# Three fixed expert tiles instead of two, and small moves among the attention steps, in a fused attention and mixture-of-experts kernel

## The chip, the cores and the metric

The kernel runs on one core of a Trainium2 chip. The metric is the device time of one execution in microseconds. PE is the matrix engine (PEld its weight loads), DVE the vector engine, ACT the scalar engine, POOL GpSimd, and SP the engine that issues most transfers.

## The reference

Three stages follow one another. In the attention stage each head projects q and k by `w_phi`, subtracts the row maximum of the absolute value, takes exp of both signs, and forms the linear attention quotient. The output, 4608 tokens by 512, feeds a top-1 mixture of eight experts behind a skip score, and that feeds a feed-forward layer.

```python
kv = np.einsum('bhsf,bhsd->bhfd', k_p, v)
z = np.sum(k_p, axis=2)
num = np.einsum('bhsf,bhfd->bhsd', q_p, kv)
den = np.einsum('bhsf,bhf->bhs', q_p, z)[..., None] + 1e-06
...
do_compute = x @ w_skip > 0
e_idx = np.argmax(xc @ w_gate, axis=1)
h = np.maximum(xc[mask] @ w1[e], 0.0)
out = xc + gate_w * (h @ w2[e])
...
h = x @ w_in
return (h - np.tanh(h)) @ w_out
```

How many tokens an expert gets depends on the inputs, which are drawn from a fixed seed.

## The kernel before, in words

The instructions of each engine stand in the order in which the program is written; nothing reorders them.

**Attention** (L695 to L787) runs 32 steps, numbered 0 to 31: a step is half the tokens of a pair of batches for one pair of heads, and eight steps finish a pair of batches. In step i the next step's keys are projected (`project(n, "k")`, L699), then the maximum is subtracted on DVE (`shift`, L250), the queries are transposed, keys and values multiplied (L305), and the key sums turned into columns (`key_value_1`, L319). The key sums themselves are eight adds a step on POOL (`key_sum`, L277 to L280), made one step ahead. Then come the next queries' projection, `key_value_t` (L327, into the same PSUM tile `kvb`), and the numerators (L343); DVE divides a step later. Both projections write one PSUM tile, `proj`, from a pool with one buffer, so each waits for the shift before it. Every second step also turns a slice of 64-bit weights into 32-bit ones (`narrow`, on DVE, ACT and POOL).

**Routing** of a pair of batches is spread over the eight steps after it, called phases. Phase 1 picks the expert, phase 2 computes the gate and the rank (`route_gate`, `route_rank`, ending in a scan, `cum`, L420, and three small operations), phase 3 counts (`route_count`, two matmuls into `kvb` at L451 and L452, two adds on DVE) and computes slots. Phases 3, 4 and 5 store the token rows into per-expert segments, three indexed stores a phase (`scatter`, L473, on POOL's queue). The last pair's routing comes after attention.

**First expert.** In step 28 (`first_expert`, L499) the expert with most tokens so far is chosen, so that its first 256 rows can be run while the last pair is still being routed. Its weights, `raw`, are split into a high part (ACT, `wh`) and a remainder (`wl`), quarter by quarter (`wsplit`, L98); in steps 29 to 31 the remainders stand on POOL.

**Fixed stage** (L855 to L901). Two tiles of 128 rows run in straight code: `up` is 24 matmuls in two halves of 512 columns, `relu_t` transposes and splits, `down` is 24 matmuls. Among them stand the last pair's gate, rank, count, slots and nine indexed stores, a table of the tiles left (`block_table`, on DVE), and the load of the loop's first rows.

**Loop** (L899). Each remaining tile is one turn; the number of turns is read from the table. A turn multiplies a tile, transposes the next tile's rows (L106) and loads the one after it. At an expert's first tile its weights are split. Then the feed-forward layer follows (L1000, L1016).

## Time and profile before

| | |
|---|---|
| runs of the kernel before, median of 3 | 1479.0 us (1476.55 to 1480.41) |
| profiled execution | 1478.13 us |
| its span, first to last instruction | 1476.4 us |
| granted PE clock, mean over the span | 0.973 of full |
| busy: PE, DVE, ACT, POOL | 1402.8 us (95%), 699.8 us (47%), 556.1 us (38%), 394.8 us (27%) |

A row of a timeline is one run of like instructions: its start, its duration, the engine and line, what it writes and reads, and in brackets how long the engine had been idle and what released it. Busy time of PE is not time at full rate, so the granted clock has to be read beside it. PE can work at full clock (1.00) or at half.

### The profile page before, as it was taken

The numbers are of one execution on the slowest core, as the hardware profiler recorded it, in microseconds if no ns is written. First come the engines' busy times: TensorE is split into PE (matmuls) and PEld (weight loads), VectorE is DVE, ScalarE is ACT, GpSimd is POOL, SyncE is SP. The second block draws the span as 40 slices with busy tenths as digits, with TensorE's granted clock in tenths as the row PEclk, the third lists the DMA queues.
The fourth block names the chain that finished last, engine by engine and source line by source line (L and its number), as shares of the span: only waits on it lengthen the run. The fifth ranks groups of instructions, "written<-read, shape, count | busy, mean of one in ns | idle before, by whom it ended". The sixth has DMA issues, their size and how long they took to land.

```text
span 1476.4 us, 26209 instructions
## 1 busy us (share of the span) xinstructions
PE 1402.8 (95%) x9733; PEld 1157.2 (78%) x9733; DVE 699.8 (47%) x1081; ACT 556.1 (38%) x911; POOL 394.8 (27%) x417
## 2 busy tenths in 40 slices
PE   6999999998999999869999999999999999999998
PEld 5887787876778777748888888888888888888886
DVE  4788787786624453557852322323223232232322
ACT  4676565655313241436642222322223222222321
POOL 4776866868601120252330100101001010000000
PEclk9999999999899999978999999999999999999999
DMA  5753765846641422334330010101001010000000
GB/s 176 181 190 126 263 218 175 270 147 211 237 164 39 153 84 101 124 132 169 123 115 0 20 39 0 57 1 57 0 0 58 0 57 1 0 29 1 29 0 30
DMA packets 53875, 139.58 MB, mean 95 GB/s; under 512 B 5776, under 2 KB 5904, under 8 KB 50704
## 3 DMA queue, kind: packets, MB, share of 16 engines
q1 hardware_dynamic: 47440, 116.16, 23.9%
q0 software_dynamic: 5760, 18.90, 4.3%
q10 hardware_dynamic: 576, 3.15, 0.5%
q8 instruction: 69, 1.13, 0.3%
q14 instruction: 30, 0.25, 0.1%
HBM read 86.00 MB, written 52.19 MB: 94 GB/s over the span
## 4 chain that ended last, share of the span: by engine, by line
PE 49%; DVE 2%; POOL 2%; issue 1%; ACT 1%; DMA 0%; POOLq 0%
PE h L1000 24%; PE acc L1016 24%; POOL raw L216 1%; PE xtr L989 1%; DVE wol L96 1%; DVE raw L213 1%; ACT woh L95 1%; POOL raw L958 0%; DVE raw L209 0%; DMA raw<-x2s,gidx 0%; DVE raw L197 0%; DVE wl L96 0%; ACT raw L205 0%; DVE raw L200 0%; DVE g L1004 0%
## 5 line engine op out<-in xcount | busy, mean ns | idle before, releaser
L1004 DVE TENSOR_TENSOR g<-h,g 128x512 f32<-128x512 f32 x144 | 99.4, 690 | 389.8 <-ACT g L1003 389.8
L1003 ACT ACTIVATE g<-h 128x512 f32<-128x512 f32 x144 | 85.7, 595 | 391.5 <-PE h L1000 391.5
L1000 PE MATMUL h<-x2Th,wh 128*128 128x512 f32 (+1 forms) x580 | 226.0, 390 | 0.0
L1000 PE MATMUL h<-x2Tl,wh 128*128 128x512 f32 (+1 forms) x580 | 225.7, 389 | 0.0
L1000 PE MATMUL h<-x2Th,wl 128*128 128x512 f32 (+1 forms) x580 | 225.7, 389 | 0.0
L1016 PE MATMUL acc<-woh,gh 128*128 128x512 f32 x576 | 225.6, 392 | 0.0
L1016 PE MATMUL acc<-woh,gl 128*128 128x512 f32 x576 | 224.3, 389 | 0.0
L1016 PE MATMUL acc<-wol,gh 128*128 128x512 f32 x576 | 224.1, 389 | 0.0
L958 POOL DMA_INDIRECT raw<-x2s,gidx x36 | 35.4, 982 | 428.2 <-PE xtr L989 416.1
L96 DVE TENSOR_TENSOR gl<-g,gh 128x512 fp32r<-128x512 f32 x144 | 101.0, 702 | 98.9 <-ACT gh L95 98.9
L95 ACT CAST gh<-g 128x512 fp32r<-128x512 f32 x144 | 89.5, 622 | 110.8 <-DVE g L1004 110.8
L1000 PEld LDWEIGHTS h<-x2Th,wh 128*128 128x128 f32 x580 | 110.0, 190 | 22.3
L1000 PEld LDWEIGHTS h<-x2Th,wl 128*128 128x128 f32 x580 | 109.9, 189 | 22.4
L1000 PEld LDWEIGHTS h<-x2Tl,wh 128*128 128x128 f32 x580 | 110.0, 190 | 22.2
L1016 PEld LDWEIGHTS acc<-woh,gl 128*128 128x128 f32 x576 | 108.1, 188 | 22.6
L1016 PEld LDWEIGHTS acc<-wol,gh 128*128 128x128 f32 x576 | 108.2, 188 | 21.9
L1016 PEld LDWEIGHTS acc<-woh,gh 128*128 128x128 f32 x576 | 108.1, 188 | 21.9
L96 POOL TENSOR_TENSOR wl<-raw,wh 128x1024 fp32r<-128x1024 f32 x25 | 65.4, 2644 | 205.8 <-PE y L832 202.6
L292 ACT ACTIVATE qp<-tq 128x640 f32<-128x640 f32 (+1 forms) x128 | 76.3, 648 | 53.8 <-PE tq L286 52.6
L343 PEld LDWEIGHTS num<-kv,qp 128*64 128x64 f32 x2304 | 87.2, 139 | 8.2 <-ACT kv L332 7.4
L343 PE MATMUL num<-kv,qp 128*64 128x74 f32 x2304 | 92.4, 234 | 0.6
L277 POOL TENSOR_TENSOR ks<-ke 128x256 f32<-128x256 f32 x64 | 52.2, 816 | 69.3 <-ACT ke L265 69.1
(193 smaller groups left out, 2243.5 us busy)
## 6 DMA issues: line engine op xcount, KB each, us to landing
raw<-in_wall_dram SPq DMA_DIRECT2D x20, 1024.0 KB, 6.4
raw<-in_w_dram SPq DMA_DIRECT2D x30, 512.0 KB, 3.6
x2s<-raw SPq DMA_DIRECT2D x24, 512.0 KB, 6.9
out_dram<-raw SPq DMA_DIRECT2D x36, 256.0 KB, 4.1
x2s<-x SPq DMA_DIRECT2D x9, 768.0 KB
k<-in_kT_dram SPq DMA_DIRECT2D x16, 320.0 KB, 2.9
q<-in_qT_dram SPq DMA_DIRECT2D x16, 320.0 KB, 4.8
v<-in_vx_dram SPq DMA_DIRECT2D x16, 320.0 KB
```

What stands on the lines that cost most here:

```text
L95: nc.scalar.copy(hi, src)
L96: eng.tensor_tensor(out=lo, in0=src, in1=hi.bitcast(F32), op=ALU.subtract)
L213: nc.vector.tensor_tensor(out=x, in0=x, in1=m, op=ALU.add)
L216: nc.gpsimd.tensor_tensor(out=x, in0=x, in1=e.bitcast(F32), op=ALU.mult)
L277: g.tensor_tensor(out=t, in0=k[:, :, 0, s], in1=k[:, :, 1, s], op=ALU.add)
L292: nc.scalar.activation(qp[h][:, s, :n], t[:, :n], AF.Exp, scale=1.0 - 2.0 * s)
L343: nc.tensor.matmul(num[r : r + 64, h, c], qp[h][:, s, slot, r : r + 64], kv[:, s, h], start=s == 0, stop=s == 1,)
L958: nc.gpsimd.indirect_dma_start(out=xg[:, t, :], out_offset=None, in_=x2s[:, :], in_offset=bass.IndirectOffsetOnAxis(ap=gidx[:, b * TB + t ...
L1000: nc.tensor.matmul(p[:, s], a[:, o : o + P], b[:, k, s], start=n == 0, stop=n == 11)
L1003: nc.scalar.activation(g, p, AF.Tanh)
L1004: nc.vector.tensor_tensor(out=g, in0=p, in1=g, op=ALU.subtract)
L1016: nc.tensor.matmul(acc[t], a[:, s], b[:, m], start=m == 0 and n == 0, stop=m == NM - 1 and n == 2)
```

## The change

1. The fixed tiles of the first expert are three (`EARLY`, `NEARLY` = 384). The third tile's rows come into `xu`; two offsets are read in place of one; the PSUM tile of the row transposes and the tiles `r`, `hh`, `hl`, `xTh`, `xTl` grow by a tile.
2. In phase 3 the counts stand behind the next queries' projection instead of ahead of the shift of the keys.
3. For the first two routed pairs the nine indexed stores are spread over phases 3 to 7 as 2, 2, 2, 2 and 1; for the third they stay at three a phase.
4. The four remainders of the first expert's up weights in steps 29 to 31 stand on DVE.
5. The fixed stage is written in another order: both halves of the second tile's up product ahead of the counts, the third tile's behind them, and the last quarter's remainder of the down weights earlier.

```diff
 W = D + 1
-NEARLY = 256
+EARLY = 3
+NEARLY = EARLY * P
 MAXT = 48
...
     bx = rctx.enter_context(tc.tile_pool(name="rows", bufs=1, side="right"))
-    xTh = bx.tile([P, 2, 4, P], F32R, name="xTh")
-    xTl = bx.tile([P, 2, 4, P], F32R, name="xTl")
+    xTh = bx.tile([P, EARLY, 4, P], F32R, name="xTh")
+    xTl = bx.tile([P, EARLY, 4, P], F32R, name="xTl")
     xr = bx.tile([P, W], F32, name="xr")
...
     forced = rt.tile([P, E], F32, name="forced")
-    head = rt.tile([P, 4], F32, name="head")
-    headi = rt.tile([P, 4], I32, name="headi")
+    head = rt.tile([P, 5], F32, name="head")
+    headi = rt.tile([P, 5], I32, name="headi")
     tab = rt.tile([P, 7], F32, name="tab")
...
         src = st[i][w]
-        p = st[i]["p" + w] = pp.tile([P, NCH * 2, NF], F32, name="proj")
+        p = st[i]["p" + w] = pp.tile([P, 12, NF], F32, name="proj")
         for c in range(4):
...
         v.tensor_scalar(
-            out=head[:, 3:4], in0=head[:, 1:2], scalar1=-float(P), scalar2=0.0, op0=ALU.add, op1=ALU.max
+            out=head[:, 4:5], in0=head[:, 1:2], scalar1=-float(P), scalar2=0.0, op0=ALU.add, op1=ALU.max
+        )
+        v.tensor_scalar(
+            out=head[:, 3:4], in0=head[:, 4:5], scalar1=float(P), scalar2=None, op0=ALU.min
         )
...
         phase = i % 8 if i >= 8 else None
-        if phase == 3:
-            routing = route_count(*routing)
         if more:
...
             load_row(xr, hrow)
-            load_row(xt, hrow2)
+            load_row(xt, hrow + offs[0])
+            load_row(xu, hrow + offs[1])
             load_part(expert_w(wv), 2)
...
             project(n, "q")
+            if phase == 3:
+                routing = route_count(*routing)
             exp_k(n, 1)
...
         else:
-            t = pp.tile([P, NCH * 2, NF], F32, name="proj")[:, :8].rearrange("p (c k) f -> p c (k f)", c=2)
-            for c, a in ((0, xr), (1, xt)):
+            t = pp.tile([P, 12, NF], F32, name="proj")
+            for c, a in ((0, xr), (1, xt), (2, xu)):
                 for k in range(4):
-                    nc.tensor.transpose(t[:, c, k * P : k * P + P], a[:, k * P : k * P + P], ident)
+                    nc.tensor.transpose(t[:, 4 * c + k], a[:, k * P : k * P + P], ident)
             split(
-                t, xTh.rearrange("p c k f -> p c (k f)"),
-                xTl.rearrange("p c k f -> p c (k f)"),
+                t.rearrange("p k f -> p (k f)"), xTh.rearrange("p c k f -> p (c k f)"),
+                xTl.rearrange("p c k f -> p (c k f)"),
             )
...
             hrow = nc.values_load(headi[0:1, 2:3], engines=[ET.SP], min_val=0, max_val=(E - 1) * CAP)
-            off = nc.values_load(headi[0:1, 3:4], engines=[ET.SP], min_val=0, max_val=P)
-            hrow2 = hrow + off
+            offs = [
+                nc.values_load(headi[0:1, j : j + 1], engines=[ET.SP], min_val=0, max_val=NEARLY - P)
+                for j in (3, 4)
+            ]
         load(n + 2, "q")
-        if phase in (3, 4, 5):
-            scatter(*routing[:2], range(phase * 3 - 9, phase * 3 - 6))
+        if phase and phase >= 3:
+            per = 2 if i < 24 else 3
+            scatter(*routing[:2], range(min(TPP, (phase - 3) * per), min(TPP, (phase - 2) * per)))
         if phase in (5, 6, 7):
...
             for j in ((), (0,), (1, 2), (3,))[i - (NS - 4)]:
-                wsplit(0, j * 1024, j * 1024 + 1024, nc.gpsimd)
+                wsplit(0, j * 1024, j * 1024 + 1024)
     divide(NS - 1)
...
-        r = bp.tile([P, 2, F], F32, name="r")
-        hh = bp.tile([P, 2, 8, P], F32R, name="hh")
-        hl = bp.tile([P, 2, 8, P], F32R, name="hl")
+        r = bp.tile([P, EARLY, F], F32, name="r")
+        hh = bp.tile([P, EARLY, 8, P], F32R, name="hh")
+        hl = bp.tile([P, EARLY, 8, P], F32R, name="hl")
         yo = bp.tile([P, D], F32, name="yo")
...
+        routing = route_pick(*route_logits(NPAIR - 1))
         wsplit(1, 0, 1024, nc.gpsimd)
         wsplit(1, 1024, 2048, nc.gpsimd)
-        routing = route_pick(*route_logits(NPAIR - 1))
         route_gate(*routing)
...
         up(0, 1)
+        up(1, 0)
+        relu_t(0, 0)
+        up(1, 1)
         routing = route_count(*routing)
         route_slot(*routing)
+        relu_t(0, 1)
         scatter(*routing[:2], range(TPP))
+        up(2, 0)
         table = block_table()
         next(table)
-        relu_t(0, 0)
-        up(1, 0)
-        relu_t(0, 1)
-        up(1, 1)
+        relu_t(1, 0)
+        wsplit(1, 3072, 4096)
+        up(2, 1)
+        relu_t(1, 1)
         next(table)
-        wsplit(1, 3072, 4096)
-        relu_t(1, 0)
-        y0 = down(0, range(4))
-        relu_t(1, 1)
+        y0 = down(0, range(8))
         seg0 = next(table)
         store_x(*routing[:2])
-        y0 = down(0, range(4, 8), y0)
+        relu_t(2, 0)
+        relu_t(2, 1)
+        y1 = down(1, range(4))
         gated(y0, xr)
         out_row(0)
-        y1 = down(1, range(2))
         table_rows()
...
         row1 = nc.values_load(mt[0:1, 1:2], engines=[ET.SP], min_val=0, max_val=RMAX)
-        y1 = down(1, range(2, 8), y1)
+        y1 = down(1, range(4, 8), y1)
         gated(y1, xt)
         load_row(xt, row1)
-        out_row(off)
+        out_row(offs[0])
+        y2 = down(2, range(8))
+        gated(y2, xu)
+        out_row(offs[1])
         tile0 = slice(0, 1)
```

How the counts stand on PE in step 27, before (`cum` is the scan, `kvb` the PSUM tile of the counts and of the keys and values):

```order
L245 MATMUL proj<-wpr,k 128x256
L451 MATMUL kvb<-cum,cst 128x8
L452 MATMUL kvb<-cum,cst 128x8
L286 MATMUL tq<-cst,dq 128x128 x4
L305 MATMUL kvb<-ke,v 64x256 x8
L305 MATMUL kvb<-kf_114,v 64x256 x2
L319 MATMUL kvb<-cst,ks 64x1 x8
L240 MATMUL proj<-wpr,q 128x128 x8
L245 MATMUL proj<-wpr,q 128x256
L327 MATMUL kvb<-wg,kvt 128x2x73 x2
```

And in the changed kernel:

```order
L246 MATMUL proj<-wpr,k 128x256
L287 MATMUL tq<-cst,dq 128x128 x4
L306 MATMUL kvb<-ke,v 64x256 x8
L306 MATMUL kvb<-kf_114,v 64x256 x2
L320 MATMUL kvb<-cst,ks 64x1 x8
L241 MATMUL proj<-wpr,q 128x128 x8
L246 MATMUL proj<-wpr,q 128x256
L452 MATMUL kvb<-cum,cst 128x8
L453 MATMUL kvb<-cum,cst 128x8
L328 MATMUL kvb<-wg,kvt 128x2x73 x2
```

The two matmuls that read `cum` moved from behind the keys' projection to behind the queries'; `proj` in both projections is the one buffer.

The same step on DVE in the changed kernel, from the gate to the counts' two adds (`mk`, `dk` are the keys' shift, `mq`, `dq` the queries'):

```order
L434 TENSOR_TENSOR nocomp<-nocomp,cst 128x9
L255 TENSOR_REDUCE mk<-proj 128x10
L259 TENSOR_TENSOR dk<-proj,mk 128x1280
L357 TENSOR_SCALAR r<-num 128x10
L358 RECIPROCAL r<-r 128x10
L366 TENSOR_TENSOR x<-num,r 128x2x4x64
L372 TENSOR_TENSOR L<-num,r 128x2x4x9
L366 TENSOR_TENSOR x<-num,r 64x128
L372 TENSOR_TENSOR L<-num,r 64x18
L455 TENSOR_TENSOR base<-kvb,runb 128x8
L456 TENSOR_TENSOR runb<-kvb,runb 128x8
L255 TENSOR_REDUCE mq<-proj 128x10
```

The adds `base` and `runb` stood ahead of `mk` and stand ahead of `mq` now; the chain that ends in `nocomp` stands ahead of `mk` as before.

DVE at the turn of steps 29 and 30, changed kernel (`wl` is a weight remainder):

```order
L255 TENSOR_REDUCE mq<-proj 128x10
L259 TENSOR_TENSOR dq<-proj,mq 128x1280
L210 SCALAR_TENSOR_TENSOR raw_74<-raw_74 128x512
L97 TENSOR_TENSOR wl_76<-raw_73,wh_75 128x1024
L255 TENSOR_REDUCE mk<-proj 128x8
L259 TENSOR_TENSOR dk<-proj,mk 128x1024
```

The remainder stood on POOL, ahead of the key sums, and stands ahead of the keys' shift on DVE now.

ACT at the start of the fixed stage, changed kernel (`ex` is the gate's exponential, `r` a relu; `h_4696` and `h_4726` are the same PSUM buffer, first and second tile):

```order
L96 CAST wh_4649<-raw_74 128x1024 x2
L441 ACTIVATE ex<-lm 128x72
L825 ACTIVATE r<-h_4696 128x512
L96 CAST wh_4649<-raw_74 128x1024
L825 ACTIVATE r<-h_4712 128x512
L825 ACTIVATE r<-h_4726 128x512
L96 CAST hh<-t_4740 128x512
```

These rows begin as they did before; the third relu followed a transposed tile's cast and follows the second relu now.

## Rows read from the trace of the kernel before

**Rows 1.** Waits of PE up to 378 us: total us, times, longest.

```profile
PE kvb L319 <- POOL ks L280: 12.2, 6, 5.0
...
PE kvb L451 <- DVE cum L420: 5.6, 3, 1.9
```

**Rows 2.** Timeline of PE: start us, us busy, engine, line, [idle before <-releaser]; steps 23, 29, 31.

```profile
277.15 0.63 PE L319 MATMUL kvb<-cst,ks 128*64 128x1 f32 x16 [1.16 <-POOL ks L280]
...
343.85 0.63 PE L319 MATMUL kvb<-cst,ks 128*64 128x1 f32 x16 [1.43 <-POOL ks L280]
...
369.25 1.02 PE L319 MATMUL kvb<-cst,ks 128*64 128x1 f32 x16 [5.03 <-POOL ks L280]
```

**Rows 3.** Timelines of PE and ACT in the fixed stage.

```profile
377.94 0.50 PE L811 MATMUL h<-wh,xTh 128*128 128x512 f32 x1
...
386.08 0.56 PE L451 MATMUL kvb<-cum,cst 128*128 128x8 f32 x2 [2.27 <-DVE cum L420]
...
411.19 0.66 PE L106 MATMUL tx<-cst,xr 128*128 128x128 f32 x4 [2.86 <-DMA xr<-xs]
...
381.84 0.26 ACT L440 ACTIVATE ex<-lm 128x72 f32<-128x72 f32 x1 [1.67 <-DVE lm L392]
```

**Rows 4.** Busy time in three stretches; PEclk is the granted clock, 1.00 full.

```profile
core 0: us, PE busy (x) PEld busy (x) DVE busy (x) ACT busy (x) POOL busy (x), PEclk, DMA share, GB/s
277.00:281.00 4.00, 3.79 (x57) 3.37 (x59) 2.29 (x5) 2.92 (x6) 1.65 (x4) 1.00 1.07 196
386.50:393.00 6.50, 6.50 (x20) 5.23 (x21) 5.99 (x22) 0.59 (x1) 4.05 (x4) 0.50 0.17 62
413.00:417.00 4.00, 4.00 (x12) 2.94 (x11) 0.19 (x1) 0.00 (x0) 0.00 (x0) 0.57 0.64 205
```

**Rows 5.** Timeline of PE, the tile loop: the same transposes one iteration apart.

```profile
432.90 0.60 PE L106 MATMUL tx<-cst,xt 128*128 128x128 f32 x4
...
445.31 0.60 PE L106 MATMUL tx<-cst,xt 128*128 128x128 f32 x4
```

**Rows 6.** Timelines of DVE and POOL where both read SBUF, and a DVE remainder alone.

```profile
302.72 0.68 DVE L209 SCALAR_TENSOR_TENSOR raw<-raw 128x512 uint32<-128x512 uint32 x1
...
302.95 1.03 POOL L277 TENSOR_TENSOR ks<-ke 128x256 f32<-128x256 f32 x1 [0.47 <-ACT ke L265]
...
304.06 0.73 POOL L278 TENSOR_TENSOR ks<-ks,ke 128x256 f32<-128x256 f32 x1
...
381.84 2.32 DVE L396 SCALAR_TENSOR_TENSOR val<-lm,cst 128x72 f32<-128x72 f32 x1
...
397.95 1.22 DVE L96 TENSOR_TENSOR wl<-raw,wh 128x1024 fp32r<-128x1024 f32 x1 [0.35 <-ACT wh L95]
```

**Rows 7.** Timeline of POOL: one indexed store, one quarter's weight remainder.

```profile
335.19 0.96 POOL L473 DMA_INDIRECT xs<-x,idx  x1 [0.30 <-issue]
...
360.65 2.39 POOL L96 TENSOR_TENSOR wl<-raw,wh 128x1024 fp32r<-128x1024 f32 x1
```

**Rows 8.** Timeline of PE, starts of the projections in steps 25 to 28.

```profile
292.87 1.16 PE L240 MATMUL proj<-wpr,k 64*128 64x128 f32 x16
...
297.88 1.16 PE L240 MATMUL proj<-wpr,q 64*128 64x128 f32 x16
...
303.38 1.16 PE L240 MATMUL proj<-wpr,k 64*128 64x128 f32 x16
...
313.41 1.16 PE L240 MATMUL proj<-wpr,k 64*128 64x128 f32 x16
...
327.94 1.16 PE L240 MATMUL proj<-wpr,k 64*128 64x128 f32 x16
```

**Rows 9.** Timeline of DVE, step 27, between the keys' two stages.

```profile
315.14 0.28 DVE L442 TENSOR_REDUCE ssum<-ex 128x9 f32<-128x72 f32 x1 [1.78 <-ACT ex L440]
...
317.31 0.17 DVE L433 TENSOR_TENSOR nocomp<-nocomp,cst 128x9 f32<-128x9 f32 x1
...
319.51 1.49 DVE L258 TENSOR_TENSOR dk<-proj,mk 128x1280 f32<-128x1280 f32 x1
```

## Prediction

> **What bounds the kernel now.** I read the chain of waits first, then PE's busy time by stretch, PE's waits up to 378 us, and last the four engines' timelines around each wait. PE is the bound nearly everywhere, so a change can gain only where PE stands still, or where it works at the lower of its two clocks (1.2 instead of 2.4 GHz). The reader should see three kinds of such places. First, in the attention steps, PE waits three times for the counts' scan (5.6 us) and six times for the key sums of POOL (12.2 us) [rows 1]. Second, it waits 5.03 us at the last step [rows 2]. Third, in the fixed stage it waits 2.27 us for the scan and 2.86 us for the first row block of the loop [rows 3]. After most of these waits the clock falls: 0.50 over 6.5 us after the 2.27, 0.57 over 4.0 us after the 2.86, but 1.00 throughout the 4 us after a wait of 1.16 us [rows 2, 4]. A fall of the usual length loses 4.0 x (1 - 0.57) = 1.7 us. I let a wait of 1.4 us or more cost its length plus 1.7, and a wait up to 1.2 its length alone.
>
> **The third fixed tile.** With the seeded inputs the expert with most tokens after three of four pairs is number 6 (576, as many as number 7, the tie going to the lower), and it ends with 781. After 256 of them 525 are left, five tiles of 128; after 384 only 397 are left, four tiles. So the loop makes one turn less. A turn is 445.31 - 432.90 = 12.41 us [rows 5], and it has the 48 large matmuls and 12 transposes that the new fixed tile has too, so work against work this is worth 0. The gain is in what the tile covers. In the fixed stage PE had 24 matmuls to run before it needed the scan; now it has 48, about 5.9 us more (383.81 - 377.94 for the first 24 [rows 3]), against a wait of 2.27. That wait and its half clock go: 2.27 + 6.5 x 0.50 = 5.5 us. From the counts to the first row block is 411.19 - 386.08 = 25.1 us, a chain of nine indexed stores on POOL, their landing and one load. Behind the counts there stood 72 large matmuls; now there stand 24 up and 72 down, 96 in all, which at the rate of the first 24 are 23.5 us at full clock, with five groups of relu transposes on top. It covers the chain but for about a microsecond either way. I take the wait and its half clock as gone: 2.86 + 1.7 = 4.6. Together **-10.1**.
>
> A new wait comes in. The second tile's first half needs the PSUM tile that the first tile's relu on ACT has to read, and ahead of that relu ACT waits for lm and computes ex: at 381.84, 3.9 us after the first matmul [rows 3]. The last remainder of the up weights now stands on DVE ahead of the division (1.22 [rows 6]), and POOL's two 2.4 us remainders [rows 7] can hold lm as they held val for 2.32 [rows 6]. So ex comes some 6.5 us after the first matmul, the relu ends 0.6 later, and PE is through its 24 matmuls at 5.9. The bounds are 0 and 2.5 us of waiting; I take 1.5, long enough for the clock to fall: 1.5 + 1.7 = **+3.2**.
>
> **Indexed stores over five steps.** One store holds POOL 0.96 + 0.30 = 1.26 us [rows 7]. Four of the six waits for key sums belong to the two pairs whose stores are spread: 12.2 - 1.43 - 5.03 = 5.7 us [rows 1, 2], and three of the four are long enough for the clock to fall. Two stores in place of three put POOL 1.26 us earlier at the first sum, which leaves 0.2 to 0.5 of a wait like the 1.43. With six stores in two steps POOL's queue ended some 1.5 us late; with four it is 2.5 us shorter, so little should be carried over to the second sum. I leave 0.4 on each of the four: gain 5.7 - 1.6 + 3 x 1.7 = 9.2; some of the wait may hide a little slack, so **-9.0**. Bounds: -10.8 if no wait is left, -4 if the clock still falls each time.
>
> **The counts behind the query projections.** The matmul that waited is moved, but what was late is the vector chain, and something else stands behind it. In step 27 DVE waits 1.78 us for ex of ACT and ends the chain at 317.31 + 0.17 = 317.48 [rows 9]. Only then comes the key's shift, 2 x 1.49, done at 320.5. The query projection writes the one PSUM tile that this shift reads, and it is due 297.88 - 292.87 = 5.01 us into a step, here at 318.42 [rows 8]. So PE waits 2.1 us there instead of 1.87 (5.6 / 3) at the counts [rows 1]. The two small matmuls keep their 0.4; the clock falls as before. Behind them the keys' projection through kvb waits for DVE's two adds on the same PSUM tile, about 0.6 (two operations of 0.17, as the one in [rows 9], and the hand-over, an estimate). The step costs 2.1 + 0.4 + 0.6 + 1.7 = 4.8 over a clean step of 303.38 - 292.87 = 10.51, and it cost 327.94 - 313.41 - 10.51 = 4.0 before [rows 8]: +0.8, three times, **+2.4**. Bounds: 0, if the adds hide, and -12 for all three if nothing took the wait's place.
>
> **The splits on DVE.** Before, one remainder of 2.39 us stood on POOL ahead of the last two key sums [rows 7], and PE waited 5.03 [rows 2]. Taking it away alone gives -2.4. But the three remainders that now run on DVE read SBUF twice, and so do the key sums. A POOL sum took 1.03 instead of 0.73 where a DVE operation of 0.68 with two SBUF inputs had begun 0.23 ahead of it [rows 6]: it stood until that one was done. The Trainium skill, page "SBUF — State Buffer", section "Who interferes with whom", states it as a rule: a VectorE instruction with two SBUF inputs and a GpSimd instruction that reads SBUF exclude each other, and the second to come waits for the whole of the first. These rows agree with it. Three remainders of 1.22 then hold POOL's queue for up to 3.7, of which I take 3.4 (each can begin a little before the sum it displaces ends): -2.4 + 3.4 = **+1.0**. Without the exclusion it would be -2.4, and the sum below 3.4 less. The first of the three also stands ahead of a key shift and delays a query projection by about 1.2; that is covered, since PE waits later for POOL anyway (5.03). If POOL were on time it would show.
>
> **At nothing:** one more small DVE operation and one more register load for the head (SP is idle there); one more row load on SP in step 30, 0.6 us of issue ahead of the second-half weights, whose first use is behind PE's last numerators; the pick of the last pair ahead of the splits, which changes no engine's order.
>
> **Sum.** -10.1 + 3.2 - 9.0 + 2.4 + 1.0 = -12.5. The profiled execution took 1478.1, so 1465.6; the median of the runs, 1479.0, stands 0.9 above it, and I forecast **1466**.
>
> **Rivals.** *POOL is free.* The exclusion doesn't reach the key sums, and DVE is in time for ex: the end gives -2.4, and the 3.2 go too: 1466 - 3.4 - 3.2 = 1459. For it: DVE has long idle stretches in the last step. Against: [rows 6]. Chance 0.20. *The counts' wait really goes*: query projections start on time, 4.0 a step: 1466 - 2.4 - 12 = 1452. Against: [rows 9] with the one PSUM tile. Chance 0.08. *No turn is saved*: the first expert still takes five: +12.4, 1478, no change. It would need more than 896 tokens. Chance 0.03. *Slower: five waits a pair.* If POOL falls behind at each of the five steps with stores, each wait reaching 1.4 and so letting the clock fall, ten waits cost 10 x 3.1 = 31 in place of the 1.6 that I leave: 1466 + 29 = 1495. It decides once POOL's queue of each step ends 1.4 us late. Against: with six stores in two steps it did so once, with four it has 2.5 us less to do. Chance 0.03. *My forecast* keeps 0.66.
>
> **How the numbers follow.** My own case lies between 1459 and 1472 by its bounds (the new waits 0 to 2.5 with or without the clock, the stores -10.8 to -4). Down to 1456 it takes in the free POOL and half of the counts' rival. So 1456 to 1472. A measurement of this kernel can tell about 0.3% from no change, 4.4 us. Faster by more: my case, the free POOL and the counts, nearly whole, 0.93. Within: the turn not saved, and a small part of mine, 0.04. Slower: 0.03.
>
> **What would show it.** Right: one pair of tile transposes fewer in the loop (16 turns, not 17); no wait at the scan in the fixed stage, but one of 1 to 2 us at the third group of twelve up matmuls, released by ACT; steps 13, 15 and 21 near 11 us at full clock; in steps 11, 19 and 27 a wait of about 2 us at the query projection, released by DVE; POOL's last key sums stretched beyond 0.73 and PE's last wait still near 5. Wrong: steps 11, 19, 27 near 10.5, a last wait under 3, a fall of the clock in all of steps 12 to 17, or a wait over 2 us at the first row block of the loop.

## The result, and the profile after

The changed kernel took 1463.97 us, the median of four runs (1460.43 to 1466.79), beside 1479.45 for the kernel before: a ratio of 0.9897, with a 95% interval of 0.9875 to 0.992. The forecast was 1466. In a second set of runs, made later for the experiments, the same kernel took 1471.09 (1466.63 to 1472.20) beside 1476.87: 0.9952 (0.9936 to 0.9969). It is faster by more than 0.3% both times, but by 1.0% once and by 0.5% the other time. Why it differs by itself is half of what the experiments show.

The profiled execution of the first set took 1460.43 us with a span of 1458.6, at a mean granted clock of 0.98 (0.973 before). PE was busy 1392.7 us (95%), POOL 388.7. These are PE's waits up to 378 us in the changed kernel (us in total, times, longest), which answer to [rows 1]:

```profile
PE proj L241 <- issue: 14.3, 5, 4.5
PE kvb L320 <- POOL ks L281: 7.4, 6, 3.9
...
PE kvb L328 <- ACT kvt L312: 2.7, 2, 2.2
PE kvb L328 <- DVE runb L456: 1.6, 3, 0.5
```

The six waits for POOL's key sums fell from 12.2 to 7.4 us, and 3.9 of what is left is the last one. The wait for the scan is gone from the list. In its place stand three waits of the queries' projection (L241), which are in the first row, and three of 0.53 us for `runb`. A wait for `kvt` of 2.2 us is new, and the prediction did not have it.

The last wait on POOL, PE in step 31, against the third of [rows 2]:

```profile
362.89 1.02 PE L320 MATMUL kvb<-cst,ks 128*64 128x1 f32 x16 [3.89 <-POOL ks L281]
```

PE in step 11 of the changed kernel (start us, us busy, engine, line, [idle before <-releaser]):

```profile
138.62 1.39 PE L241 MATMUL proj<-wpr,q 64*128 64x128 f32 x16 [2.18 <-issue]
...
141.23 0.57 PE L453 MATMUL kvb<-cum,cst 128*128 128x8 f32 x2
142.34 1.34 PE L328 MATMUL kvb<-wg,kvt 128*128 128x146 f32 x4 [0.53 <-DVE runb L456]
```

And DVE ahead of it, same columns; the first row is the gate's sum, which waits for `ex`, the second the scan that the counts read:

```profile
133.23 0.28 DVE L443 TENSOR_REDUCE ssum<-ex 128x9 f32<-128x72 f32 x1 [1.78 <-ACT ex L441]
...
134.80 0.31 DVE L421 TENSOR_TENSOR_SCAN cum<-cst,oh 128x72 f32<-128x72 f32 x1
...
135.51 1.48 DVE L255 TENSOR_REDUCE mk<-proj 128x10 f32<-128x1280 f32 x1
137.03 1.49 DVE L259 TENSOR_TENSOR dk<-proj,mk 128x1280 f32<-128x1280 f32 x1
```

The profile names no releaser for the 2.18 us, but DVE's shift of the keys ends at 138.52, 0.1 us before PE goes on. It is the wait that the prediction described: 2.1 us at the projection, 0.6 behind the counts. Steps 19 and 27 have it too, 2.19 and 2.27 us.

The fixed stage and the entry of the loop, PE in the changed kernel, against [rows 3]:

```profile
372.05 0.50 PE L820 MATMUL h<-wh,xTh 128*128 128x512 f32 x1 [0.61 <-DVE xTl L97]
...
378.69 0.50 PE L820 MATMUL h<-wh,xTh 128*128 128x512 f32 x1 [0.78 <-ACT r L825]
...
409.54 0.60 PE L107 MATMUL tx<-cst,xr 128*128 128x128 f32 x4
```

The waits for the scan (2.27) and for the first row block (2.86) are gone, and the new wait for the first relu is 0.78 us. From the first matmul to the first row block it takes 37.49 us, where it took 33.25; from there to the last row block of the loop 213.83, where it took 227.40. One turn of 12.41 us [rows 5] has left the loop.

The steps of attention whose length changed, in us, from one keys' projection to the next (worked out from PE's timelines; a clean odd step takes 10.51, a clean even one 9.66). The last two columns are an experiment that is told below:

| step | before | changed | changed, 2nd set | counts put back | the same, 2nd set |
|---|---|---|---|---|---|
| 11 | 14.67 | 16.52 | 18.16 | 13.20 | 14.52 |
| 13 | 13.79 | 10.51 | 11.80 | 10.99 | 11.20 |
| 15 | 13.57 | 10.94 | 11.36 | 10.95 | 14.29 |
| 19 | 14.66 | 13.77 | 16.53 | 13.30 | 13.18 |
| 21 | 13.46 | 10.85 | 11.16 | 10.81 | 11.37 |
| 23 | 11.76 | 10.95 | 10.90 | 10.96 | 11.05 |
| 25 | 10.51 | 14.65 | 13.45 | 14.03 | 14.27 |
| 27 | 14.53 | 13.85 | 16.62 | 13.28 | 13.28 |
| 28 | 9.95 | 9.66 | 13.29 | 9.95 | 11.30 |
| 29 | 13.61 | 12.19 | 10.98 | 13.59 | 12.38 |
| start of step 30 | 351.50 | 343.54 | 354.46 | 340.57 | 347.89 |

Steps 13, 15, 21 and 23 are what the spread stores gained. Steps 11, 19, 27 and 28 make up the 10.9 us between the two profiled executions of the changed kernel. Step 25 is the new wait; the 14.29 of step 15 in the last column comes from the same operation of ACT, as told below.

### The profile page after: what moved, and what is told of

Its sections match the earlier page's. It is cut to its first block, busy times and chain, and to the rows that moved or that the text cites. A ratio compares the mean times of both kernels' runs of the same rounds, so it can differ in the third digit from the quotient of the medians.

```text
span 1458.6 us, 26066 instructions
## 1 busy us (share of the span) xinstructions
PE 1392.7 (95%) x9733; PEld 1150.6 (79%) x9733; DVE 701.2 (48%) x1083; ACT 555.6 (38%) x910; POOL 388.7 (27%) x413
## 4 chain that ended last, share of the span: by engine, by line
PE 49%; DVE 3%; POOL 2%; ACT 1%; issue 1%; DMA 0%; POOLq 0%
PE h L1015 24%; PE acc L1031 24%; POOL raw L217 1%; PE xtr L1004 1%; DVE wol L97 1%; DVE raw L214 1%; ACT woh L96 1%; DVE raw L210 0%; POOL raw L973 0%; DVE raw L198 0%; DVE wl L97 0%; ACT raw L206 0%; DMA raw<-x2s,gidx 0%; DVE raw L201 0%; DVE g L1019 0%
## 5 line engine op out<-in xcount | busy, mean ns | idle before, releaser
L97 POOL TENSOR_TENSOR wl<-raw,wh 128x1024 fp32r<-128x1024 f32 x21 | 56.3, 2708 | 201.0 <-PE y L841 191.1
L841 PE MATMUL y<-wl,hh 128*128 128x512 f32 x152 | 62.5, 411 | 9.4 <-DVE wl L97 9.4
```

Of the source, the lines that this page charges most:

```text
L97: eng.tensor_tensor(out=lo, in0=src, in1=hi.bitcast(F32), op=ALU.subtract)
L841: nc.tensor.matmul(y, a[:, c, m], b[1][:, m * D : m * D + D], start=m == 0 and a is hh and b is wh, stop=m == 7 and a is hl,)
```

## The experiments

Twelve runs follow, in four sets: ten new kernels, the changed kernel again, and one of the ten again. All kernels of a set ran beside the kernel before on one chip, and ratios are against it.

| kernel | median us | before beside it | ratio | 95% interval |
|---|---|---|---|---|
| counts put back | 1458.29 | 1478.62 | 0.9866 | 0.9851 to 0.9880 |
| splits put back on POOL | 1461.78 | 1478.62 | 0.9877 | 0.9856 to 0.9897 |
| stores alone | 1470.43 | 1478.62 | 0.9943 | 0.9926 to 0.9959 |
| third tile alone | 1466.64 | 1478.62 | 0.9913 | 0.9899 to 0.9927 |
| gate's sum later | 1457.74 | 1477.47 | 0.9872 | 0.9853 to 0.9892 |
| two places for the words | 1464.82 | 1477.47 | 0.9926 | 0.9908 to 0.9944 |
| both of these | 1455.16 | 1477.47 | 0.9849 | 0.9829 to 0.9869 |
| changed kernel again | 1471.09 | 1476.87 | 0.9952 | 0.9936 to 0.9969 |
| ex early, counts back | 1459.42 | 1476.87 | 0.9881 | 0.9859 to 0.9903 |
| ex early | 1462.57 | 1476.87 | 0.9896 | 0.9873 to 0.9919 |
| four edits together | 1451.64 | 1476.87 | 0.9824 | 0.9810 to 0.9837 |
| counts put back, again | 1466.17 | 1477.55 | 0.9923 | 0.9907 to 0.9938 |

### One part alone

**Third tile alone.** The changed kernel with counts, stores and splits as they were before.

> The kernel before with one part of the change alone: three fixed tiles and the order of the fixed stage that goes with them; counts, stores and splits are as before. Prediction's sum for this part: -10.1 + 3.2 = -6.9, so 1472.5. By the changed kernel's trace the part should give about -9 to -10 (fixed stage and the loop's start without the two long waits and their half clock, one wait of 0.8 in their place), so 1469 to 1471. With the first expert's remainders on POOL, lm can come later than in the changed kernel and the new wait for relu reach 1.5 or more. Rival (the third tile only moves a turn from the loop to the fixed stage): within 2 us of 1479.

Measured: 1466.64, that is 12.0 us below the kernel before, 2 to 3 us more than I expected. These are all its waits between 352 and 420 us:

```profile
PE kvb L320 <- POOL ks L281: 5.1, 1, 5.1
PE h L818 <- ACT xTh L96: 0.7, 1, 0.7
PE h L818 <- DVE xTl L97: 0.6, 1, 0.6
PE kvb L328 <- ACT kvt L312: 0.5, 1, 0.5
```

No wait for relu, none for the scan, none for a row block. Its span is 10.1 us shorter: +0.4 up to step 30, +0.8 from there to the first up matmul (four transposes more), +3.2 in the fixed stage, -12.3 in the loop, -0.2 between, and -2.0 after the loop. The 2 us after the loop, where the program is the same, come from its very end. SP issues the last four stores of the output in 2.26 us in all twelve executions here that have three fixed tiles, and in 4.88 and 4.86 in the kernel before and the stores alone. From the last matmul to the end of the span it takes 4.4 us in place of 7.4; 0.7 of this gain is lost again ahead of the last matmul. SP in the kernel before, and in the third tile alone:

```profile
1468.10 4.88 SPq L1051 DMA_DIRECT2D out_dram<-raw  x4
...
1460.96 2.26 SPq L1064 DMA_DIRECT2D out_dram<-raw  x4
```

So some 3 of the 12 us come from the last four stores, for which the prediction had no term. Why they are issued faster stays open.

**Stores alone.** The kernel before with this edit only:

```diff
-        if phase in (3, 4, 5):
-            scatter(*routing[:2], range(phase * 3 - 9, phase * 3 - 6))
+        if phase and phase >= 3:
+            per = 2 if i < 24 else 3
+            scatter(*routing[:2], range(min(TPP, (phase - 3) * per), min(TPP, (phase - 2) * per)))
```

> The kernel before with one part of the change alone: the indexed stores of the second and the first pair over five steps, two in each. My theory: 9 to 10 us faster than the kernel before (1469 to 1471), steps 13, 15 and 21 between 10.5 and 11.0 us long, and step 25 with the same new wait for the transposed kvt as in the changed kernel (some 4 us, which is then part of the sum, so 1470 rather than 1469). Rival (five waits a pair): slower than 1479. Rival (the waits go, but the clock falls elsewhere): within 2 us of 1479.

Measured: 1470.43, 8.2 us less, as expected. Steps 13, 15, 21 and 23 took 11.01, 10.94, 10.81 and 10.94 us, together 8.9 less than before. Step 25 took 11.85 in place of 10.51, so the new wait is there, but it cost 1.3 and not 4 in this execution. Both rivals are out.

### What the splits on DVE do to POOL

```diff
             for j in ((), (0,), (1, 2), (3,))[i - (NS - 4)]:
-                wsplit(0, j * 1024, j * 1024 + 1024)
+                wsplit(0, j * 1024, j * 1024 + 1024, nc.gpsimd)
```

> The changed kernel with one part undone: the four splits of the first expert's up weights have their remainders on POOL again, in steps 29 to 31. My theory (DVE's remainders stand in the way of POOL's key sums): POOL's key sums are 0.73 to 1.03 us again except behind a remainder, the last wait on POOL is about 5 us, and from the start of step 30 to the first up matmul it takes 1 to 2 us less than the 28.5 us of the changed kernel. The fixed stage however may wait longer for lm, since more of POOL's remainders run. In all 0 to 2 us faster than the changed kernel. Rival (without the exclusion the splits on DVE are a gain): 2 to 4 us slower.

Measured: 1461.78, 2.2 us under the changed kernel's first median, in another set, so no more than a hint. The traces say more. POOL in the changed kernel, the last step's key sums:

```profile
356.50 1.59 POOL L280 TENSOR_TENSOR ks<-ks,ke 128x256 f32<-128x256 f32 x1
358.17 1.59 POOL L281 TENSOR_TENSOR ks<-ks,kf 128x256 f32<-128x256 f32 x1
359.71 0.72 POOL L278 TENSOR_TENSOR ks<-ke 128x256 f32<-128x256 f32 x1
```

and DVE beside it (two remainders in one row):

```profile
355.71 3.46 DVE L97 TENSOR_TENSOR wl<-raw,wh 128x1024 fp32r<-128x1024 f32 x2 [2.04 <-ACT wh L96]
```

Each sum that meets a remainder takes 1.59 instead of 0.73, and the two remainders take 3.46 instead of 2 x 1.22: each stands until the other is done. That is the rule which the prediction quoted from the Trainium skill, page "SBUF — State Buffer", section "Who interferes with whom", and these rows agree with it. With the remainders on POOL the same place reads:

```profile
353.81 2.38 POOL L97 TENSOR_TENSOR wl<-raw,wh 128x1024 fp32r<-128x1024 f32 x1
356.14 0.72 POOL L278 TENSOR_TENSOR ks<-ke 128x256 f32<-128x256 f32 x1
```

One remainder of 2.38 in POOL's queue has been exchanged for three sums that are each 0.86 longer, 2.6 in all (the third is in step 30). From the start of step 30 to the first up matmul it takes 28.33 us with the splits on POOL and 28.51 with them on DVE; I had expected 1 to 2 less. But this stretch differs from one execution to the next: with the remainders on DVE it took 26.4 to 28.5 us in the nine executions here, with them on POOL 27.2, 28.3 and 26.4, and the clock cost it 5.1 us in the first execution of the changed kernel and 3.4 in this one. So neither a gain nor a loss is shown there. In four of the nine (counts put back, gate's sum later, two places, both of these) the wait moved: PE waited 3.0 to 3.1 us for the query projection of step 30, and only 0.8 to 1.9 for the last key sums. PE in the gate's sum later:

```profile
348.25 2.08 PE L241 MATMUL proj<-wpr,q 64*128 64x128 f32 x16 [3.10 <-issue]
```

DVE's first remainder waited there for its high part from ACT until 343.90 and took 1.86 us, and the shift of the keys behind it ended at 348.15, 0.1 us before PE went on.

The other cost is in the fixed stage: with the fourth remainder on POOL there is no wait for relu, and the stage is 1.04 us shorter (36.45 against 37.49). This one is firm: 36.45 in all three executions with the remainders on POOL, 37.5 to 37.8 in all nine with them on DVE. DVE then held `val` for 2.32 us behind POOL's remainders, and no longer `lm`, on which ex and the relu wait.

### Counts, and what they wait for

**Counts put back.** The changed kernel with `route_count` ahead of `shift(n, "k")` again:

```diff
         phase = i % 8 if i >= 8 else None
+        if phase == 3:
+            routing = route_count(*routing)
...
             project(n, "q")
-            if phase == 3:
-                routing = route_count(*routing)
```

> The changed kernel with one part undone: the two counting matmuls stand again ahead of the key shift, in front of the transposes. My theory: what is late is DVE's chain behind ex of ACT, and the counts' place only decides which matmul waits for it. PE then waits 1.7 to 2.0 us at the counts in steps 11, 19 and 27 (5.2 to 6.0 in all), no longer 2.2 at the query projection and 0.53 behind it, and the time stays within 2.5 us of the changed kernel's (median 1464), either way. By the prediction's own sum it is 2.4 us faster. Rival: the move took the wait away, and undoing it costs up to 12 us (1476).

Measured: 1458.29. The waits were 1.9 to 2.0 us at the counts, as expected; the time was not within 2.5 us of the changed kernel's. In this execution the clock did not fall once at these waits. PE's busy time in step 11 with the counts put back (stretch, its length, PE busy, granted clock, DMA):

```profile
core 0: us, PE busy (x), PEclk, DMA share, GB/s
130.00:134.00 4.00, 2.13 (x24) 1.00 0.31 93
134.00:138.00 4.00, 3.85 (x51) 1.00 0.13 29
```

The changed kernel in the same step:

```profile
138.00:142.00 4.00, 3.19 (x22) 0.68 0.01 2
142.00:146.00 4.00, 3.66 (x33) 0.50 0.01 2
146.00:150.00 4.00, 4.00 (x76) 0.97 0.60 116
```

The loss is 4.0 x (0.32 + 0.50 + 0.03) = 3.4 us, twice the 1.7 that I had put on a fall. Yet in step 19 of the same execution, after 2.19 us of waiting in the same place, there was none:

```profile
222.00:226.00 4.00, 1.93 (x32) 1.00 0.44 138
226.00:230.00 4.00, 3.34 (x30) 1.00 0.00 0
```

**The changed kernel again, and the counts put back again.** Both as they were.

> The changed kernel once more, unchanged, on the chip of the three runs beside it. In the first look the changed kernel's waits at the query projections let the clock fall in step 11 but not in steps 19 and 27, although they were equally long (2.2 us). My theory: whether a wait of about 2 us lets the clock fall differs from execution to execution, so the steps 11, 19 and 27 will be between 13.7 us (no fall) and 16.6 us (fall), not all as before, and the median lies between 1460 and 1467. Rival: the falls belong to places in the program; then the same three steps have the same lengths as in the first look (16.5, 13.8, 13.9).

> The kernel with the counts put back ahead of the key shift once more, unchanged. In its first look the clock fell after none of the three waits at the counts (2.0 us each; steps 11, 19 and 27 took 13.2 us), in the kernel before and in the third tile alone after all three (14.7 us). My theory: a wait of about 2 us lets the clock fall in some executions and not in others, wherever the counts stand. Then the three steps lie between 13.2 and 16.2 us, at least one of them with a fall, and the median between 1457 and 1466. Rival: with the counts ahead and the stores over five steps the clock does not fall at all; then 13.2 us three times again and 1456 to 1460, and putting the counts behind was a loss of 5 us or more by itself.

Measured: 1471.09 and 1466.17; the first is above the range that I expected, and so is its step 11. The changed kernel's three steps now all had a fall (18.16, 16.53, 16.62 us), and the longest one, in step 11, cost 4.0 x (0.49 + 0.50 + 0.29) = 5.1 us. Its second execution, step 11:

```profile
138.00:142.00 4.00, 3.61 (x22) 0.51 0.00 0
142.00:146.00 4.00, 3.86 (x36) 0.50 0.02 6
146.00:150.00 4.00, 4.00 (x66) 0.71 0.61 126
```

The counts put back had one fall in three (14.52, 13.18, 13.28), of 1.7 us, after a wait of 1.85 in step 11 and none after 1.86 in step 19:

```profile
135.51 0.39 PE L452 MATMUL kvb<-cum,cst 128*128 128x8 f32 x2 [1.85 <-DVE cum L421]
...
225.57 0.39 PE L452 MATMUL kvb<-cum,cst 128*128 128x8 f32 x2 [1.86 <-DVE cum L421]
```

```profile
136.00:140.00 4.00, 4.00 (x24) 0.57 0.02 6
...
226.00:230.00 4.00, 3.85 (x48) 1.00 0.09 18
```

Both rivals are out: the falls belong neither to the place nor to the length of the wait alone. Nor does it take two sets of runs: side by side in the first set, the four runs of the changed kernel lie at 1460.43 and 1461.79 with a mean granted clock of 0.980, and at 1466.14 and 1466.79 with 0.975 and 0.976. The Trainium skill, page "TensorE: Matmul & The Clock Gate", section "What's actually happening", says that the chip watches PE's activity by a clock of its own, which does not start with the kernel, so that the point at which the clock changes differs between runs; these executions agree in that one and the same wait is followed by different falls, but that this is the reason no run here can show. What went with the place is the length of a fall. Ahead of the key shift a fall lost 1.7 us in all seven cases of the kernel before, the third tile alone and this run, with the stores alone twice 1.7 and once 3.4. Behind the projections nine of twelve waits (the changed kernel twice, the splits put back, and two places for the words) were followed by a fall, and each lost 3.4 or 5.1 us. What makes them longer there was not tested; a second wait, the 0.53 us for `runb`, follows only in that place. Against the kernel before, the counts ahead of the shift are 0.003 better in both pairs of sets, some 4.4 us. As the two kernels of a pair never ran in the same set and their intervals touch, that size is not settled, but the sign came out the same twice.

**What makes the counts late.** The gate's sum, which waits for ex, goes one step later on DVE:

```diff
         if phase == 2:
-            route_gate(*routing)
+            ex = gate_exp(routing[3])
+            gx = routing[1]
             routing = route_rank(*routing)
         if phase == 3:
+            gate_sum(gx, ex)
             route_slot(*routing)
```

> The changed kernel with one edit: in each pair's third step the sum and the reciprocal of the gate, which wait for ex of ACT, stand one step later on DVE, ahead of the slots; ex itself stays where it was. Same computation. My theory: DVE's wait for ex is the whole cause of the waits at the query projections of steps 11, 19 and 27. Without it the key shift is done 1.8 to 2.5 us earlier, the waits of 2.2 us go to 0.3 or less, and with them the fall of the clock: those three steps are 10.5 to 11.2 us long in place of 16.5, 13.8 and 13.9. In all 8 to 12 us faster than the changed kernel, 1452 to 1456. Rival: DVE is late by its own work, and the wait stays above 1 us; then 0 to 3 us faster.

Measured: 1457.74, 1.7 above what I expected. The waits of 2.2 us are gone and there was no fall: steps 11, 19 and 27 took 12.23, 12.22 and 12.31. But a part came back. PE in steps 11 and 12 of this kernel:

```profile
137.21 1.16 PE L241 MATMUL proj<-wpr,q 64*128 64x128 f32 x16 [0.65 <-PE kvb L320]
...
139.87 0.76 PE L328 MATMUL kvb<-wg,kvt 128*128 128x146 f32 x4 [0.53 <-DVE runb L462]
...
149.15 1.16 PE L241 MATMUL proj<-wpr,q 64*128 64x128 f32 x16 [0.73 <-PE kvb L320]
```

DVE's shift still ends 0.65 us late, by DVE's own work, and the moved sum makes the next shift late: step 12 took 11.16 in place of 9.66. So the gate, which is the wait for ex and the sum behind it, was most of the wait, not all of it. The next two runs tell ex from the sum.

**ex early.** Then ex was put behind the pick, one step earlier, where ACT is free, and its sum behind the ranks; once with the counts where the change has them, once with the counts put back.

```diff
         if phase == 1:
             routing = route_pick(*routing)
+            ex = gate_exp(routing[3])
         if phase == 2:
-            route_gate(*routing)
+            gx = routing[1]
             routing = route_rank(*routing)
+            gate_sum(gx, ex)
```

> The same early ex, with the counts where the change has put them, behind the query projections. My theory: steps 11, 19 and 27 are 11.3 to 11.5 us long (10.51, the two matmuls 0.4, and the wait of 0.53 for DVE's sums, which stays), so 0.5 us a step slower than with the counts ahead: 1452 to 1456. With the chain on time the place of the counts is worth less than 2 us either way. Rival: moving the counts is a gain by itself once ex is early; then this is over 2 us faster than the run with the counts ahead.

> The changed kernel with two edits: in each pair's second step ex is computed on ACT right behind the pick, and its sum stands behind the ranks on DVE in the third step; and the counts stand ahead of the key shift again. Same computation. My theory: with ex long done DVE's chain ends some 1.8 us earlier; no wait at the counts (below 0.3 us), none at the query projections, and none for the counts' sums behind them; steps 11, 19 and 27 are 10.9 to 11.2 us long, steps 12, 20 and 28 at most 10.0, and in none of them does the clock fall. About 1451 to 1454 where the kernel with the counts put back took 1458. Rival: ACT's ex delays the transposed queries in the second step, and a wait of 1 us or more comes there; then no gain.

Measured, in the set of the changed kernel's second execution (1471.09): 1462.57 and 1459.42, both above what I expected (1452 to 1456, 1451 to 1454). Making ex early, with its sum behind the ranks, is worth 8.5 us there, and the intervals lie apart. But little of this is the wait itself. The step lengths were missed: 12.92, 13.01 and 13.01 in the one (11.3 to 11.5 expected), 12.07, 13.98 and 11.97 in the other (10.9 to 11.2). With the counts behind, the waits at the query projections shrank from 2.2 us to 1.33, 1.42 and 1.42. DVE and PE in step 11 of that kernel:

```profile
131.72 0.72 DVE L421 TENSOR_TENSOR_SCAN cum<-cst,oh 128x72 f32<-128x72 f32 x1
...
137.24 1.16 PE L241 MATMUL proj<-wpr,q 64*128 64x128 f32 x16 [1.33 <-issue]
```

DVE no longer waits 1.78 us for ex, but it now does the ranks while POOL's key sums still run (until 133.92), and small operations that took 0.31 and 0.17 us behind those sums (the scan, `nocs`) take 0.72 and 0.58 beside them. So of the 2.2 us, having ex early took away 0.8, moving the sum a step later as well (the run before) another 0.7, and 0.65 is DVE's other work. The rest of the gain is the clock: no fall followed the waits of 1.33 to 1.42 us, where the falls in the same three steps of the changed kernel's second execution lost some 12 us.

With the counts ahead, another wait took the place, PE in step 11 and in step 19:

```profile
135.25 1.95 PE L306 MATMUL kvb<-ke,v 128*64 128x256 f32 x16 [0.93 <-ACT qp L293]
...
221.87 3.61 PE L306 MATMUL kvb<-ke,v 128*64 128x256 f32 x16 [1.27 <-ACT qp L293]
```

In step 19 the clock fell behind it: the same 16 matmuls took 3.61 in place of 1.95 us, and the fall lost 1.7. So a wait of 1.27 us can be followed by a fall, where I had let that begin at 1.4. The profile names ACT, but DVE's timeline has the likelier releaser, the last of the counts' sums on the same PSUM tile, which in step 11 ends 0.1 us before:

```profile
134.71 0.22 DVE L453 RECIPROCAL x<-ssum 128x9 f32<-128x9 f32 x1
...
134.98 0.17 DVE L462 TENSOR_TENSOR runb<-kvb,runb 128x8 f32<-128x8 f32 x1
```

The gate's sum now stands ahead of `base` and `runb`. With the sum behind them the wait should shrink; that was not run. The 3.2 us between the two kernels lie inside their overlapping intervals.

### The new wait in step 25

ACT in the changed kernel, steps 24 and 25:

```profile
289.94 0.76 ACT L206 ACTIVATE raw<-raw,bias 128x512 f32<-128x512 uint32 x1 [6.21 <-issue]
...
292.07 0.38 ACT L312 COPY kvt<-kvb 128x256 f32<-128x256 f32 x1
```

L206 writes the words that the last transfer to `ffw` still reads. Here the profile names no releaser; at 180.58 and 265.23 us, where the same operation stood 2.54 and 2.10 us, it names that transfer. Everything behind it on ACT comes late, and PE waits 2.17 us for `kvt` at 292.50. In the kernel before, the same operation stood 1.49 us and nobody waited for it. In other executions it stood in step 15 (counts put back, second set: 5.17 us) or in step 17, here with ex early:

```profile
200.32 0.76 ACT L206 ACTIVATE raw<-raw,bias 128x512 f32<-128x512 uint32 x1 [5.19 <-DMA ffw<-raw]
```

PE then waited 1.14 us for `kvt` and step 17 took 12.78 in place of 10.51. The edit gives the words two places in turn:

```diff
-        nc.sync.dma_start(ffw[:, j * 512 : j * 512 + 512], w_tmp[2])
+        nc.sync.dma_start(ffw[:, j * 512 : j * 512 + 512], w_x[j % 2])
...
-                narrowing = narrow(w_in, *w_tmp)
+                narrowing = narrow(w_in, *w_tmp, w_x[wi % 2])
```

> The changed kernel with one edit: the narrowed words (the tile that the store of the last expert's weights reads) lie alternately in two places of SBUF, so ACT does not wait for the store before. Same computation. My theory: the new wait of step 25 (2.2 us for the copy of kvt, behind an ACT operation that stood 6.2 us) comes from that store alone; step 25 is 10.5 to 10.6 us long in place of 14.65, and the kernel 3 to 4 us faster than the changed one in executions that show the wait. If the wait also explains why the runs of the changed kernel lie in two groups 5 us apart, the groups go as well. Rival: DVE, which waited 0.57 us for an indexed store, is late too, and the wait stays over 1 us: no difference.

Measured: 1464.82, and ACT no longer stands there:

```profile
289.05 0.78 ACT L206 ACTIVATE raw<-raw,bias 128x512 f32<-128x512 uint32 x1
```

Step 25 took 10.51 us, as in the two other kernels with two places below; with one place and the spread stores it took 10.75 to 14.65 in all nine executions. So the single place is shown to be the cause. In this execution the clock fell in all three steps with counts (16.56, 16.47, 16.51), and the median, 0.9926 of the kernel before, lies between the two of the changed kernel, which did not run in this set. On top of the later gate, in the same set, the edit is worth more:

> The changed kernel with both edits, the gate's sum one step later and two places for the narrowed words. If the two waits are independent, the gains add: 11 to 16 us faster than the changed kernel, 1448 to 1453. If the clock falls at another wait instead, or if POOL becomes late, less than either edit's gain alone on top of the other.

Measured: 1455.16, 2.6 us less than the later gate alone (1457.74; the ranges just touch, 1452.36 to 1455.73 and 1455.45 to 1458.57). Less than the sum that I expected.

### The fastest version

ex early, counts put back, two places for the words, and the remainders on POOL.

> The candidate for the fastest version: the changed kernel with ex early, the counts ahead of the key shift, two places for the narrowed words, and the first expert's remainders on POOL. Same computation. My theory: on top of the early ex with the counts ahead, step 25 loses its 2 to 4 us of wait and half clock, and the remainders are worth 0 to 2 us: 1446 to 1451. Rival: these edits only move a wait, as the two places for the narrowed words alone did; then 1451 to 1454 as without them.

Measured: 1451.64 (1449.25 to 1454.22), 0.9824 of the kernel before, faster than both kernels and 19.5 us below the changed kernel in the same set. That is 0.6 above my range and inside the figure that I gave the rival, 1451 to 1454. But that figure stood for the kernel without the last two edits, and it took 1459.42 (1454.79 to 1464.86) in the same set; the ranges lie apart, so the rival's claim, that these edits only move a wait, is out. Which of the two edits gave how much of the 7.8 us was not separated. PE's waits in it up to 370 us show what could still go, the wait at the keys and values that the profile puts down to ACT:

```profile
PE kvb L307 <- ACT qp L294: 3.1, 3, 1.3
```

## Why the prediction was right, and where it was not

The forecast of 1466 lies 2.0 us above the first set's median and 5.1 below the second's. The direction and most of the waits were right; that the sum came so close is in part luck. The third tile alone gained 5.1 us more than its two terms together (12.0 against 10.1 - 3.2 = 6.9), 3 of them by the last four stores, which I did not foresee. Against that stand the counts, some 2 us dearer than their term by the two pairs of sets, the stores, 0.8 less than theirs, and the wait of step 25, which was missing.

**Third tile (-10.1).** Right in kind: one turn less, both waits and their half clock gone. In the trace of the third tile alone the loop, the fixed stage and the way to it gave 12.3 - 3.2 - 0.8 = 8.3, less than the 10.1, although no long wait was left; the 2 us after the loop were not foreseen and make up for it. Alone the part measured -12.0.

**The wait for relu (+3.2).** Mis-sized: 0.78 us, and no fall of the clock (0.77 to 1.05 us in all nine executions with the remainders on DVE). It does not come from the third tile alone: it hangs on the fourth remainder on DVE, which the prediction names, since none of the three kernels with three tiles and the remainders on POOL has it.

**Stores (-9.0).** Right: -8.2 alone, with the wait of step 25 in it. The remaining waits in steps 15, 21 and 23 are 0.26 to 0.35 us where I had left 0.4.

**Counts (+2.4).** The mechanism was right, to the waits of 2.2 and 0.53. The step that failed is the one on the clock: "I let a wait of 1.4 us or more cost its length plus 1.7". Waits of 2.2 us cost nothing extra, 3.4 or 5.1 us, by the execution. So the term lies between about +1 (no fall either way: a step of 13.77 with 9.66 behind it, against 13.20 with 9.96, 0.27 three times) and some 5, as the two pairs of sets had it.

**Splits (+1.0).** The exclusion is right, but I had it as 3.4 us of standing time, and it was 3 x 0.86 = 2.6. What the end of attention lost or gained is not settled, as the same kernel's executions differ there by 1.7 us. The last wait on POOL, which was to stay near 5, was 3.89 and 3.21 in the changed kernel; and where POOL was on time, the first remainder did show at the query projection of step 30, as the prediction said it would. What is firm is the relu's wait, 1.0 us.

**Missing.** Step 25. I priced what the change does to POOL's queue, not what it does to the transfers: ACT's operation came to need the place of the words before the store to `ffw` had read it. 2.2 us of waiting, and a step 4.1 us longer in the first execution. Why the store is late is not settled. Steps 12 to 24 are some 11 us shorter there; but in the second sets of the changed kernel and of the counts put back they are only 4.8 and 5.7 us shorter, and step 25 was nearly as long. And with the spread stores, in every execution, an indexed store leaves POOL within 1.1 us of this one (at 279.66 and 280.74 us in the changed kernel); in the two kernels without them none is near.

Of the rivals, the free POOL and the counts' wait that really goes did not come: the sums are stretched, and the wait is there in every execution. A turn was saved, and five waits a pair were not seen.

## What to carry to other kernels

When a matmul waits, moving the matmul only chooses which of the next ones waits; find the first late instruction on the engine that releases it (here a sum that waited for an exponential) and take it out of the way; making its input early gave only part of that back here, because the operations behind it then ran beside another engine's and took longer. A wait of 1.3 to 2 us on PE should be priced as a spread, from its own length to that and some microseconds of half clock, and two sets of runs of one kernel can then differ by half a per cent; compare only kernels that ran side by side, over several executions. When a change shortens steps or moves transfers, look at every tile that a transfer still reads: a single place for it can become the next wait.

## What the runs showed of the hardware that was not expected

The same wait in the same place of the same program (2.2 us, steps 11, 19 and 27) was followed by 3.4, 0 and 0 us of lost clock in one execution and by 5.1, 3.4 and 3.4 in another. And in step 13 of the second execution ACT began its copy of `kvt` at 165.46, 1.6 us after the last matmul ahead of it had ended (163.87), where in the first it began 0.1 us after it (162.78). The same instructions stand ahead of it, and the cause stays open. PE and ACT in the second execution:

```profile
163.29 0.58 PE L320 MATMUL kvb<-cst,ks 128*64 128x1 f32 x16
...
165.46 0.37 ACT L312 COPY kvt<-kvb 128x256 f32<-128x256 f32 x1 [3.12 <-remote]
```
